# Attention and an expert layer: x times w_in from 7 block products of 384 tokens instead of 8

## The chip, the cores and the metric

The kernel runs on one core of a Trainium2 chip. The metric is the device time of one execution in microseconds. Engines are named as in the profile: PE (TensorE matmul), PEld (its weight load), DVE (VectorE), ACT (ScalarE), POOL (GpSimd), SP (SyncE, which issues the DMAs here).

## What is computed

```python
def _attn_ref(q, k, v, f):                       # batch 8, heads 8, 576 positions, 64 wide
    scores = scale * np.matmul(q, k.transpose(0, 1, 3, 2))
    cum = np.cumsum(np.log(np.clip(f, 0.0001, 1.0)), axis=-1)
    scores = np.where(causal, -1e9, scores + cum[..., :, None] - cum[..., None, :])
    attn = np.exp(scores - np.max(scores, axis=-1, keepdims=True))
    return np.matmul(attn / (np.sum(attn, axis=-1, keepdims=True) + 1e-09), v)

def _moe_ref(x, w_in, w_out):                    # x 4608 x 512, w_in 512 x 2048, w_out 2048 x 512
    h = x @ w_in
    sp = np.maximum(h, 0.0) + np.log1p(np.exp(-np.abs(h)))
    g = h * erf(sp)
    return g @ w_out
```

The attention's output, written as 4608 tokens of 512 values, is `x`. The weights arrive as 64-bit floats.

## The kernel before

The program has two stages. **The attention** works on half heads `t` = 0 to 63, five of them in flight, and writes the transposed output to the DRAM buffer `xt_d`. **The expert layer** (class `Moe`) follows; its first four units are already placed in the last attention steps. This change leaves the attention's own work alone.

Every number that enters a matmul of the expert layer is held as two float32r parts, a high part (`xh`, `wh`, `gh`) and the rest (`xl`, `wl`, `gl`), and a product is three matmuls: high x high, high x rest, rest x high. DVE or ACT makes the high part by a copy that rounds; POOL makes the rest by a subtraction.

A *unit* is one chunk of 512 tokens and 128 of the 2048 features. There are 9 chunks and 16 feature groups, so 144 units. `up` (L130) makes `h` of a unit in a PSUM bank, `ph`, from 12 matmuls of 512 columns (4 parts of the 512 inputs x 3). ACT then takes softplus of `ph` (L135) and erf (L138), DVE multiplies the result by `ph` (L144, one operand in PSUM) and rounds it (L146, a cast from SBUF to SBUF), and POOL makes the rest (L147). `down` (L168 to L170) then multiplies two units at a time with `w_out`: 24 matmuls of 512 columns into four PSUM banks `y`, which collect a visit's features. softplus and erf have different tables in ACT, so that each pair of units loads two tables (the load belongs to L138 and to L218).

The order on each engine is the order in which the code is written. `Moe.step` writes one unit: its `up`, then the `down` of an earlier pair, erf, softplus and the gates of earlier units, and the loads of `x`. Four PSUM banks hold `ph`, four hold `y`.

The weights are converted from 64-bit floats in pieces of 128 x 512 values: an Abs on ACT (L292), then DVE operations on SBUF (L296, L301, L303, L306), a cast (L309) and POOL's subtraction (L310). 16 pieces are converted in the attention stage, 16 beside the first part of the expert layer, two conversion steps in each `step`; the load of the next piece is issued when the last step of a piece is done (L282, through the SP queue). All converted weights stay in SBUF. The first five chunks are visited twice, each time with half of the features; their half sums go through DRAM (`part_d`).

## Time and profile before

| | us |
|---|---|
| median of 3 runs | 1117.68 (1116.02 to 1117.72) |
| the profiled execution | 1114.65 |
| its span, first to last instruction | 1112.9 |
| PE busy | 1102.9 (99% of the span) |
| DVE, ACT, POOL busy | 566.8, 694.2, 518.6 |
| first and last `up` matmul (L130) start | 312.0 and 1092.5 |

The profile is of one execution, and 1.8 us of its time lie outside its span. Rows of groups read: line, engine, operation, written tile <- read tiles, shape, count | busy us, mean ns of one | idle time before them, and what ended it. Rows of the timeline read: start, duration, engine, line. A query for one line or tile gives minimum, median and maximum in ns.

### The profile page before, as it was taken

The numbers are of one execution on the slowest core, as the hardware profiler recorded it, in microseconds if no ns is written. First come the engines' busy times: TensorE is split into PE (matmuls) and PEld (weight loads), VectorE is DVE, ScalarE is ACT, GpSimd is POOL, SyncE is SP. The second block draws the span as 40 slices with busy tenths as digits, with TensorE's granted clock in tenths as the row PEclk, the third lists the DMA queues.
The fourth block names the chain that finished last, engine by engine and source line by source line (L and its number), as shares of the span: only waits on it lengthen the run. The fifth ranks groups of instructions, "written<-read, shape, count | busy, mean of one in ns | idle before, by whom it ended". The sixth has DMA issues, their size and how long they took to land.

```text
span 1112.9 us, 19392 instructions
## 1 busy us (share of the span) xinstructions
PE 1102.9 (99%) x7096; PEld 914.8 (82%) x7096; DVE 566.8 (51%) x1475; ACT 694.2 (62%) x1303; POOL 518.6 (47%) x664
## 2 busy tenths in 40 slices
PE   8999999999999999999999999999999999999998
PEld 7888888888878888888888888888888888888887
DVE  6888888888855575764323332233223222313322
ACT  4888888888878697885554544554454445345442
POOL 4778787878945354354243242342232232223211
PEclk9999999999999999999999999999999999999999
DMA  8788787888613224131122032030011000000101
GB/s 289 215 259 265 238 258 250 261 250 252 213 63 104 78 77 133 62 109 57 46 87 95 19 114 95 19 114 38 1 38 39 1 24 30 24 19 1 39 1 38
DMA packets 57726, 120.03 MB, mean 108 GB/s; under 512 B 4768, under 2 KB 20128, under 8 KB 57632
## 3 DMA queue, kind: packets, MB, share of 16 engines
q1 hardware_dynamic: 57632, 118.80, 33.2%
q8 instruction: 56, 0.92, 0.3%
q14 instruction: 38, 0.31, 0.1%
HBM read 94.52 MB, written 24.26 MB: 107 GB/s over the span
## 4 chain that ended last, share of the span: by engine, by line
PE 96%; DVE 1%; issue 1%; ACT 1%; POOL 0%; POOLq 0%; DVEq 0%; ACTq 0%
PE ph L130 35%; PE y L170 12%; PE y L168 12%; PE y L169 12%; PE s L380 9%; PE o L461 8%; PE t L434 8%; DVE pr L400 1%; PE s L384 1%; PE idle L493 0%; ACT pr L412 0%; ACT pt L443 0%; POOL pr L422 0%; DVE pt L441 0%; POOL c L367 0%
## 5 line engine op out<-in xcount | busy, mean ns | idle before, releaser
L147 POOL TENSOR_TENSOR gl<-e,gh 128x512 fp32r<-128x512 f32 x144 | 186.2, 1293 | 410.0 <-DVE gh L146 403.2
L130 PE MATMUL ph<-xh,w 128*128 128x512 f32 x1152 | 367.3, 390 | 0.6 <-DVE st L400 0.6
L135 ACT ACTIVATE e<-ph 128x512 f32<-128x512 f32 x144 | 86.0, 598 | 278.9 <-PE ph L130 160.9
L130 PEld LDWEIGHTS ph<-xh,w 128*128 128x128 f32 x1152 | 216.2, 188 | 45.7 <-PE o L461 0.7
L144 DVE TENSOR_TENSOR e<-e,ph 128x512 f32<-128x512 f32 x144 | 98.3, 682 | 298.0 <-ACT e L138 298.0
L130 PE MATMUL ph<-xl,w 128*128 128x512 f32 x576 | 224.1, 389 | 0.0
L168 PE MATMUL y<-w,gh 128*128 128x512 f32 x576 | 224.1, 389 | 0.0
L169 PE MATMUL y<-w,gh 128*128 128x512 f32 x576 | 224.1, 389 | 0.0
L170 PE MATMUL y<-w,gl 128*128 128x512 f32 x576 | 224.1, 389 | 0.0
L422 POOL TENSOR_SCALAR pr<-pr,st 128x576 f32<-128x576 f32 (+4 forms) x320 | 165.5, 537 | 46.3 <-DVE st L418 38.4
L412 ACT ACTIVATE pr<-pr,st 128x576 f32<-128x576 f32 (+3 forms) x320 | 176.8, 558 | 4.8 <-DVE st L400 4.8
L400 DVE CUSTOM_DVE_ANT_0 pr<-s,c 128x576 f32<-128x576 f32 (+3 forms) x320 | 136.6, 486 | 37.2 <-PE s L384 28.9
L146 DVE CAST gh<-e 128x512 fp32r<-128x512 f32 x144 | 102.0, 708 | 57.8 <-PE y L169 44.3
L168 PEld LDWEIGHTS y<-w,gh 128*128 128x128 f32 x576 | 108.3, 188 | 22.5
L130 PEld LDWEIGHTS ph<-xl,w 128*128 128x128 f32 x576 | 108.2, 188 | 22.5
L170 PEld LDWEIGHTS y<-w,gl 128*128 128x128 f32 x576 | 107.9, 187 | 22.5
L169 PEld LDWEIGHTS y<-w,gh 128*128 128x128 f32 x576 | 108.1, 188 | 22.3
L380 PE MATMUL s<-k,q 64*128 64x320 f32 (+4 forms) x768 | 108.5, 407 | 2.1 <-DVE st L400 2.1
L434 PE MATMUL t<-ident,pr 128*128 128x128 f32 x800 | 104.4, 276 | 2.2 <-DVE pt L441 1.1
L443 ACT COPY pt<-t 128x512 f32<-128x512 f32 x128 | 73.6, 577 | 48.4 <-PE t L434 48.4
L461 PE MATMUL o<-pt,v 128*64 128x128 f32 (+1 forms) x1920 | 102.5, 259 | 0.0
L461 PEld LDWEIGHTS o<-pt,v 128*64 128x64 f32 x1920 | 93.7, 137 | 9.5 <-DVE st L400 4.9
(56 smaller groups left out, 1089.5 us busy)
## 6 DMA issues: line engine op xcount, KB each, us to landing
v<-in_vp_dram SPq DMA_DIRECT2D x32, 576.0 KB, 6.5
c<-cum_d SPq DMA_DIRECT2D x62, 288.0 KB, 5.3
xr<-xt_d SPq DMA_DIRECT2D x28, 512.0 KB, 3.4
q<-in_q_dram SPq DMA_DIRECT2D x32, 320.0 KB, 3.5
k<-in_k_dram SPq DMA_DIRECT2D x32, 288.0 KB, 4.0
xt_d<-xo SPq DMA_DIRECT2D x32, 288.0 KB, 5.6
wraw<-in_w_in_dram SPq DMA_DIRECT2D x16, 512.0 KB, 5.6
wraw<-in_w_out_dram SPq DMA_DIRECT2D x16, 512.0 KB, 4.4
```

The lines of the kernel that those rows point to most:

```text
L130: nc.tensor.matmul(out=ps, lhsT=w[:, kd, fs], rhs=x[:, kd], start=kd == 0 and n == 0, stop=kd == KD - 1 and n == 2)
L146: nc.vector.tensor_copy(out=gh, in_=e_)
L147: nc.gpsimd.tensor_tensor(out=gl, in0=e_, in1=gh.bitcast(F32), op=ALU.subtract)
L168: nc.tensor.matmul(out=y[tb], lhsT=gh[:, cs], rhs=wh, start=first, stop=False)
L169: nc.tensor.matmul(out=y[tb], lhsT=gh[:, cs], rhs=wl, start=False, stop=False)
L170: nc.tensor.matmul(out=y[tb], lhsT=gl[:, cs], rhs=wh, start=False, stop=last)
L380: nc.tensor.matmul(out=s[j][:, at:at + k1 - k0], lhsT=q[h, PAD + START[i]:PAD + END[i]], rhs=k[h, k0:k1], start=i > 0, stop=i not in (0, 3))
L400: nc.vector.tensor_tensor_reduce(out=to[:, ::-1] if j else to, in0=score, in1=decay_, scale=-0.125, scalar=BIG, op0=ALU.add, op1=ALU.min, ...
L412: nc.scalar.activation(out=seg, in_=seg, func=AF.Exp, bias=st[:, 0, j, m:m + 1], scale=-1.0, accum_out=st[:, 1, j, m:m + 1])
L422: nc.gpsimd.tensor_scalar(out=seg, in0=seg, scalar1=st[:, 2, j, m:m + 1], scalar2=1.0, op0=ALU.mult, op1=ALU.mult)
L434: nc.tensor.transpose(out=b[:, n * P:(n + 1) * P], in_=probs[t][:, at:at + P], identity=ident)
L461: nc.tensor.matmul(out=o[h, to:to + width], lhsT=v[:, ch, h], rhs=pt[:, at[j]:at[j] + width], start=n == 0, stop=n == len(parts) - 1, skip ...
```

## The change

The product x times w_in of two blocks of 384 tokens, two halves of the 512 inputs and two groups of 128 features is made by Strassen's scheme: 7 products of blocks instead of 8, on sums and differences of the blocks of x and of w_in. What follows is in the words of the new code.

A *block* is a pair of 384-token blocks with half of the features (1024); there are 6 pairs and 2 halves, first all pairs with the first half, then all with the second, so 12 blocks. A block has four *steps* (`k` = 0 to 3, `n` = 0 to 47 over all), each with 256 features. A step has seven *slots*. In slot `i` PE makes product `i`, 6 matmuls of 384 columns (2 input parts x 3), and then 5 (in the last slot 6) of the 36 `y` matmuls of 512 columns of step `n - 2`.

- `product` uses two PSUM banks in turn; products 2, 5 and 6 are added on to 0, 3 and 4 in their bank, and so must wait until `consume` has read what was there.
- `consume` brings each result to SBUF. After products 0 and 2 that is a copy on ACT, after the others an addition on DVE of the bank and an SBUF tile. The four quarters of `h` end up in SBUF.
- After product 0, ACT takes the last two softplus and the four erf of step `n - 1`; after product 1, DVE and POOL make its four gates. The multiplication in `gate` now has both operands in SBUF.
- `load_x`, `x_sum`, `split_x` and `last_sum` make the seven sums of x of the next block, each of 128 x 768 values, in steps 2 and 3 of a block and step 0 of the next. Each has one buffer for both parts.
- `weight_work` converts the weights and makes the seven sums of w_in. Ten of the 32 pieces are converted in the attention stage; the other 22 are written as 108 small work items, and `filler` places them in the slots of steps 2 to 18 by the table `FILL`. The second half's parts are stored to DRAM (`wi_d`, `wo_d`), and `reload` reads them back over the first half's in steps 20 to 25. The tile for a loaded piece (`raw`) has one buffer; the next load is issued in `join`.
- All half sums of `y` of the first half go through DRAM (`part_d`); there are six `y` banks.
- The first 14 products (steps 0 and 1) lie in the last four attention steps, between transposes.

```diff
-TB = 512
+TB = 384
+PRODUCTS = [(0, 0, True), (4, 1, True), (1, 0, False), (3, 1, True), (5, 0, True), (2, 1, False), (6, 0, False)]
+XSLOT = [0, 5, 1, 4, 6, 2, 3]
+FILL = [[1, 0, 1, 1, 2, 1, 2], [1, 0, 1, 1, 1, 1, 2], [0, 0, 0, 0, 0, 1, 2]]
+YCUT = [0, 5, 10, 15, 20, 25, 30, 36]
...
+    def x_sum(self, v, j):
+        t, sub = self.t[v], self.nc.gpsimd
+        if j == 0:
+            sub.tensor_tensor(out=t[4], in0=t[2], in1=t[3], op=ALU.add)
+        else:
+            sub.tensor_tensor(out=t[2], in0=t[0], in1=t[2], op=ALU.subtract)
+
+    def split_x(self, v, i):
+        t, r = self.t[v], XSLOT[i]
+        src = t[{0: 0, 5: 0, 1: 1, 4: 4, 6: 2, 2: 1, 3: 3}[r]]
+        x = self.x_tile(v, r)
+        h, l = x[:, 0], x[:, 1]
+        if i in (3, 4):
+            nc.scalar.copy(out=h, in_=src)
+        else:
+            nc.vector.tensor_copy(out=h, in_=src)
+        eng = nc.vector if i in (0, 4) else nc.gpsimd
+        eng.tensor_tensor(out=l, in0=src, in1=h.bitcast(F32), op=ALU.subtract)
+        if i == 0:
+            nc.vector.tensor_tensor(out=t[0], in0=t[4], in1=t[0], op=ALU.subtract)
+
+    def last_sum(self, v):
+        self.nc.vector.tensor_tensor(out=t[1], in0=t[1], in1=t[0], op=ALU.subtract)
...
+    def product(self, n, i):
...
+        w, bank, first = PRODUCTS[i]
+        ps = self.m[bank]
+        w, x = self.wi[v // NPAIR, k][:, w], self.x[v, XSLOT[i]]
+        for kd in range(2):
+            ws = slice(kd * P, kd * P + P)
+            for j, (wp, xp) in enumerate(((0, 0), (0, 1), (1, 0))):
+                nc.tensor.matmul(out=ps, lhsT=w[:, wp, ws], rhs=x[:, xp, kd], start=first and kd == 0 and j == 0,
+                                 stop=kd == 1 and j == 2 and i in (1, 2, 5, 6), skip_group_check=True)
...
+    def consume(self, n, i):
+        ps = self.m[PRODUCTS[i][1]]
+        if i == 0:
+            nc.scalar.copy(out=self.s1, in_=ps)
+        elif i == 1:
+            nc.vector.tensor_tensor(out=self.u2, in0=ps, in1=self.s1, op=ALU.add)
+        elif i == 2:
+            nc.scalar.copy(out=self.h_tile(n, 0), in_=ps)
+        elif i == 3:
+            nc.vector.tensor_tensor(out=self.u4, in0=ps, in1=self.u2, op=ALU.add)
+        else:
+            q, base = {4: (3, self.u4), 5: (1, self.u2), 6: (2, self.u2)}[i]
+            nc.vector.tensor_tensor(out=self.h_tile(n, q), in0=ps, in1=base, op=ALU.add)
...
+    def gate(self, n, q):
+        e, h = self.e.pop((n, q)), self.h.pop((n, q))
+        nc.vector.tensor_mul(e, e, h)
...
+        nc.vector.tensor_copy(out=gh, in_=e)
+        nc.gpsimd.tensor_tensor(out=gl, in0=e, in1=gh.bitcast(F32), op=ALU.subtract)
...
+    def step(self, n):
...
+        if gates:
+            self.softplus(n - 1, 0)
+            self.softplus(n - 1, 1)
+        if after and k == 2:
+            self.load_x(v + 1)
+        for i in range(7):
+            if up:
+                self.product(n, i)
+                self.consume(n, i)
+            if gates and i == 0:
+                for q in (2, 3):
+                    self.softplus(n - 1, q)
+                for q in range(4):
+                    self.erf(n - 1, q)
+            if after and k == HU - 1 and i < 2:
+                self.split_x(v + 1, i)
+            if gates and i == 1:
+                for q in range(4):
+                    self.gate(n - 1, q)
+            if up and i == (2 if gates else 5):
+                self.nc.scalar.preload_act_table_set(SOFTPLUS)
+            if after and k == HU - 1 and 2 <= i < 5:
+                if i == 3:
+                    self.last_sum(v + 1)
+                self.split_x(v + 1, i)
+            if up and v and k == 0 and i < 2:
+                self.split_x(v, 5 + i)
+            if after and k == 2 and i in (5, 6):
+                self.x_sum(v + 1, i - 5)
+            for _ in range(YCUT[i + 1] - YCUT[i]):
+                next(downs, None)
+            if n >= 2:
+                self.filler(FILL[0 if n < 5 else 1 + (k == HU - 1)][i])
...
+        for m, (a, i) in enumerate(pieces):
+            work += [lambda m=m: magnitude(m), lambda m=m: normal(m), lambda m=m: low_bits(m)]
+            if i >= 2:
+                work.append(lambda m=m: (join(m), out_parts(m)))
+            elif i == 0:
+                work.append(lambda m=m: (join(m), in_parts(m, 0, quarter(m, 0))))
+            else:
+                work += [lambda m=m: join(m), lambda m=m: [in_parts(m, 1 + f, quarter(m, f)) for f in range(2)],
+                         lambda m=m: sums(m, 0), lambda m=m: sums(m, 1)]
+                work += [lambda m=m, j=j: [in_parts(m, 3 + w, tops["t"][:, w]) for w in (j, j + 1)] for j in (0, 2)]
```

`magnitude` is the Abs on ACT, `normal`, `low_bits` (two instructions) and `join` are the DVE operations, `in_parts` and `out_parts` the cast on DVE and the subtraction on POOL, and where the piece is of the second half also two stores.

**PE.** Before, the matmuls of a pair of units stand in one piece, and so do those of `down` (the end of a `down` and the start of a unit, `ph`):

```order
L169 MATMUL y3_3_6602<-w3_108,gh31_6786 128x512
L170 MATMUL y3_3_6602<-w3_108,gl31_6787 128x512
L130 MATMUL ph36_6884<-xh4_6506,w2_107 128x512
L130 MATMUL ph36_6884<-xl4_6507,w2_107 128x512
L130 MATMUL ph36_6884<-xh4_6506,w2_107 128x512 x2
L130 MATMUL ph36_6884<-xl4_6507,w2_107 128x512
```

Now, in a step of block 9 (counted from 0), each product (`m39_*`, the banks of step 39) is six matmuls of 384 columns between five of `y9_*` of step 37:

```order
L147 MATMUL m39_1_11473<-x9_5_10927,wi1_3_9292 128x384 x6
L206 MATMUL y9_0_11353<-wo1_1_9294,gl37_1_11379 128x512
L206 MATMUL y9_1_11354<-wo1_1_9294,gh37_0_11373 128x512 x2
L206 MATMUL y9_1_11354<-wo1_1_9294,gl37_0_11374 128x512
L206 MATMUL y9_1_11354<-wo1_1_9294,gh37_1_11378 128x512
L147 MATMUL m39_0_11472<-x9_1_10964,wi1_3_9292 128x384 x6
L206 MATMUL y9_1_11354<-wo1_1_9294,gh37_1_11378 128x512
L206 MATMUL y9_1_11354<-wo1_1_9294,gl37_1_11379 128x512
```

A bank is now needed again two products later, where before a unit's bank came round after four units.

**DVE.** Before, the gates of two units stand alone on DVE for long stretches (L144 reads the bank `ph`):

```order
L144 TENSOR_TENSOR e56_7630<-e56_7630,ph56_7614 128x512
L146 CAST gh56_7700<-e56_7630 128x512
L144 TENSOR_TENSOR e57_7674<-e57_7674,ph57_7637 128x512
L146 CAST gh57_7746<-e57_7674 128x512
L196 TENSOR_TENSOR part6_0_7510<-y6_0_7506,part6_0_7510 128x512
```

Now, in the last step of a block (step 23), the sums of the next block's x (`x6_*`, `t6_*`) stand ahead of the gates of step 22:

```order
L121 CAST x6_0_9168<-t6_0_9000 128x768
L123 TENSOR_TENSOR x6_0_9168<-t6_0_9000,x6_0_9168 128x768
L125 TENSOR_TENSOR t6_0_9000<-t6_4_9004,t6_0_9000 128x768
L163 TENSOR_TENSOR sb23_9183<-m23_1_9151,sa23_9158 128x384
L121 CAST x6_5_9185<-t6_0_9000 128x768
L184 TENSOR_TENSOR e22_0_9146<-e22_0_9146,h22_0_9077 128x384
L188 CAST gh22_0_9189<-e22_0_9146 128x384
```

and, after the other three gates, between them and the additions that free the banks for products 5 and 6 (`sc23`, `h23_3`):

```order
L188 CAST gh22_3_9204<-e22_3_9162 128x384
L121 CAST x6_1_9222<-t6_1_9001 128x768
L168 TENSOR_TENSOR sc23_9237<-m23_2_9230,sb23_9183 128x384
L129 TENSOR_TENSOR t6_1_9001<-t6_1_9001,t6_0_9000 128x768
L171 TENSOR_TENSOR h23_3_9255<-m23_3_9248,sc23_9237 128x384
```

POOL's part of the same step: the rest of `x6_5` stands ahead of the four gates' rests, that of `x6_1` behind them:

```order
L123 TENSOR_TENSOR x6_5_9185<-t6_0_9000,x6_5_9185 128x768
L189 TENSOR_TENSOR gl22_0_9190<-e22_0_9146,gh22_0_9189 128x384
L189 TENSOR_TENSOR gl22_1_9195<-e22_1_9148,gh22_1_9194 128x384
L189 TENSOR_TENSOR gl22_2_9200<-e22_2_9160,gh22_2_9199 128x384
L189 TENSOR_TENSOR gl22_3_9205<-e22_3_9162,gh22_3_9204 128x384
L123 TENSOR_TENSOR x6_1_9222<-t6_1_9001,x6_1_9222 128x768
```

The additions out of PSUM, which come behind the gates in every step, have the sums of x between them and the gates in this one; `t6_1` is overwritten by DVE after POOL has read it.

**ACT.** Before, a weight piece's Abs (`wtop17`) stands behind the softplus of a unit, with a table load on either side:

```order
L218 ACT_TABLE_LOAD
L135 ACTIVATE e6_5669<-ph6_5653 128x512
L292 ACT_TABLE_LOAD
L292 ACTIVATE wtop17_5676<-wraw17_5651 128x512
L135 ACT_TABLE_LOAD
L135 ACTIVATE e7_5716<-ph7_5679 128x512
```

Now, at the change from step 8 to step 9, the Abs of piece 10 stands ahead of the softplus of step 8 (`e8_*`) and of the copy `sa9` of product 0 of step 9:

```order
L356 ACT_TABLE_LOAD
L356 ACTIVATE ltop10_6838<-lraw10_6817 128x512
L175 ACT_TABLE_LOAD
L175 ACTIVATE e8_0_6857<-h8_0_6777 128x384
L175 ACTIVATE e8_1_6859<-h8_1_6831 128x384
L160 COPY sa9_6869<-m9_0_6861 128x384
```

What waits for that copy is product 2 of step 9, which is added on in the same bank.

More of the change, by code (lines that the diff above doesn't have):

```diff
@@ L68, with __init__ @@
 class Moe:
[L75 to L77 removed]
+    def __init__(self, tc, xt_d, part_d, out, xs):
         self.tc, self.nc = tc, tc.nc
[L79 to L94 removed]
@@ L203, in more @@
-    def more(self):
-        return self.at < self.steps
-    def step(self):
-        j, n = self.at, len(self.units)
-        self.at += 1
-        if j < n:
-            self.up(j)
-            self.want_x(self.units[min(j + 5, n - 1)][0])
-        if self.downs[j]:
-            for i in range(0, len(self.downs[j]), 2):
-                self.down(self.downs[j][i:i + 2])
-        if j in self.ends:
-            for i in self.ends[j]:
-                self.erf(i)
-            self.nc.scalar.preload_act_table_set(SOFTPLUS)
-        if j < n:
-            self.softplus(j)
-        for i in self.gates[j]:
-            self.gate(i)
-        for i in self.downs[j]:
-            self.finish(i)
-        self.split_x()
-        self.load_x()
+        self.xt_d, self.part_d, self.out, self.xs = xt_d, part_d, out, xs
@@ new lines, in down @@
+    def down(self, n):
+        nc = self.nc
+        v, k = divmod(n, HU)
+        if k == 0:
+            self.y[v] = [self.ps_y.tile([P, DM], F32, name=f"y{v}_{tb}", tag=f"y{tb}") for tb in range(NTB)]
+        y, w = self.y[v], self.wo[v // NPAIR, k]
+        for tb in range(NTB):
+            token, at = divmod(tb, 3)
+            cs = slice(at * P, at * P + P)
+            for f in range(2):
+                gh, gl = self.g[n, 2 * token + f]
+                for j, (g, wp) in enumerate(((gh, 0), (gh, 1), (gl, 0))):
+                    first, last = k == 0 and f == 0 and j == 0, k == HU - 1 and f == 1 and j == 2
+                    yield nc.tensor.matmul(out=y[tb], lhsT=g[:, cs], rhs=w[:, f, wp], start=first, stop=last)
+            if k == HU - 1:
+                self.finish(v, tb)
@@ L284, in convert @@
-    def convert(u, step):
-        a, i = divmod(u, 4)
-        half, col = i // 2, slice(i % 2 * 512, i % 2 * 512 + 512)
-        raw = raws[u].rearrange("p (n w) -> p n w", w=2)
-        w0, w1_ = raw[:, :, 0], raw[:, :, 1]
-        if step == 0:
-            raws[u, 0] = top = cv.tile([P, 512], F32, name=f"wtop{u}", tag="wtop")
-            nc.scalar.activation(out=top, in_=w1_.bitcast(F32), func=AF.Abs)
-            return
-        top = raws[u, 0]
-        if step == 1:
-            nc.vector.scalar_tensor_tensor(out=top, in0=top, scalar=TINY, in1=w1_.bitcast(F32),
+    part_d = [dram.tile([P, DM], F32, name=f"part_d{c}") for c in range(NT // P)]
@@ L486, in attention_moe, with moe_products @@
         nc.sync.dma_start(out=fd[1], in_=f[0, 1].partition_broadcast(P))
-        todo = pieces[1]
+        tail = iter(i for n in range(2) for i in moe.step(n))
+        def moe_products(t, n):
+            if NH <= t < NH + 4:
+                for _ in range(n if t % 2 == 0 or n < 2 else 1):
+                    next(tail)
         def idle_products(t, n):
@@ L513, in attention_moe @@
                 load_values(p - 1)
-            if NH <= t < NH + 4:
-                moe.step()
             if there[2]:
@@ L530, in attention_moe @@
                     mask(0, slice(1, 2))
+            moe_products(t, 2)
             if there[3]:
```

377 lines of the change are left out of this document (215 added, 162 removed).

## The prediction

> **What bounds the kernel now.** I read the page first, then the stages, the chain and PE's waits.
>
> ```profile
> span 1112.9 us, 19392 instructions
> PE 1102.9 (99%) x7096; PEld 914.8 (82%) x7096; DVE 566.8 (51%) x1475; ACT 694.2 (62%) x1303; POOL 518.6 (47%) x664
> ```
> ```profile
> 343.00:1093.00 750.00, 750.00 (x3311) 621.02 (x3310) 281.48 (x410) 413.71 (x486) 260.97 (x181) 1.00 0.16 53
> ```
> ```profile
> 347.61 5.44 PE ph L130 x24
> ...
> 1087.45 5.44 PE ph L130 x24
> ```
> ```profile
> PE s L380 <- DVE st L400: 2.1, 2, 1.7
> ```
>
> PE is busy all through the expert layer, at the full granted clock (the 1.00), and the longest wait of PE anywhere is 1.7 us. From the first to the last quoted piece of the chain lie 739.84 us and 68 pairs of units, 10.88 us each. A pair has 48 matmuls of 512 columns: 226.7 ns each. So the layer costs 72 x 10.88 = 783.4 us of PE, and fewer columns are a real gain as long as PE stays fed. DVE and POOL have slack of many us here:
>
> ```profile
> DVE e L144 <- ACT e L138: 298.0, 50, 12.0
> ```
>
> **Term 1, fewer columns.** A step has 7 x 6 = 42 matmuls of 384 columns and 36 of 512; 48 steps replace the 72 pairs. No row has 384 columns. The nearest is 226.7 ns at 512: in proportion 170. The other side is the 128-column transposes:
>
> ```profile
> 203.65 1.48 PE L434 MATMUL t<-ident,pr 128*128 128x128 f32 x12
> ...
> L434 PE MATMUL t<-ident,pr x800: 270/273/328, 24.1 to 330.2; 128*128 128x128 f32 x160
> ```
>
> Twelve starts in 1.48 - 0.27 us are 110 ns each, and the line from there to 226.7 gives 188 at 384. I take 173, near the proportional end, since 110 is about the pace of loading 128 columns of weights and that hides under 170. A step is 42 x 0.173 + 36 x 0.2267 = 15.43 us, 48 are 740.5: **-42.9** (ends -49 and -13). The Trainium skill ("TensorE: Matmul & The Clock Gate", Back-to-back issue gap) gives columns / 2.4 + 2.5 ns, 162.5 ns at 384; by it this term would be -64. It gives 216 at 512 where the trace has 226.7, so the trace decides.
>
> **Who must keep pace.** Product 5 starts 5 x (6 x 0.173 + 5 x 0.2267) = 10.86 us after product 0, and needs bank 1 read by DVE (`consume` of 3), which stands behind the step's four gates. So I walk that queue, with these rows:
>
> ```profile
> L130 PE MATMUL ph<-xh,w 128*128 128x512 f32 x1152 | 367.3, 390 | 0.6 <-DVE st L400 0.6
> L147 POOL TENSOR_TENSOR gl<-e,gh 128x512 fp32r<-128x512 f32 x144 | 186.2, 1293 | 410.0 <-DVE gh L146 403.2 <-PE ph L130 3.4 <-PE t L434 3.4
> L118 POOL TENSOR_TENSOR xl<-xr,xh 128x1024 fp32r<-128x1024 f32 x28 | 67.9, 2425 | 53.4 <-ACT xh L117 52.4 <-DVE st L418 1.1
> L198 DVE COPY yo<-y 128x512 f32<-128x512 f32 x32 | 21.7, 689 | 42.7 <-PE y L170 31.5 <-DMA part_d<-yo 11.3
> L470 DVE COPY xo<-o 128x256 f32<-128x256 f32 x32 | 12.7, 398 | 0.0
> L138 ACT ACT_TABLE_LOAD x72 | 92.4, 1283 | 1.3
> L181 ACT COPY yo<-y 128x256 f32<-128x256 f32 x4 | 1.5, 372 | 11.3 <-DVE yo L179 11.3
> L443 ACT COPY pt<-t 128x512 f32<-128x512 f32 x128 | 73.6, 577 | 48.4 <-PE t L434 48.4
> ```
> ```profile
> L303 DVE SCALAR_TENSOR_TENSOR wraw<-wraw x32: 692/702/1667, 40.9 to 513.2; 128x512 int32<-128x512 int32 x32
> L306 DVE SCALAR_TENSOR_TENSOR wtop<-wtop,wraw x32: 681/698/1664, 45.5 to 513.9; 128x512 int32<-128x512 int32 x32
> ...
> L146 DVE CAST gh<-e x144: 426/430/1461, 328.6 to 1098.7; 128x512 fp32r<-128x512 f32 x144
> ```
> ```profile
> 357.57 1.15 ACT L138 ACTIVATE e<-e 128x512 f32<-128x512 f32 x2
> ...
> 356.37 1.31 POOL L147 TENSOR_TENSOR gl<-e,gh 128x512 fp32r<-128x512 f32 x1 [2.78 <-DVE gh L146]
> 356.57 1.66 DVE L303 SCALAR_TENSOR_TENSOR wraw<-wraw 128x512 int32<-128x512 int32 x1
> ...
> 359.33 0.68 DVE L144 TENSOR_TENSOR e<-e,ph 128x512 f32<-128x512 f32 x1
> 359.50 1.29 POOL L310 TENSOR_TENSOR w<-wtop,w 128x512 fp32r<-128x512 f32 x1 [1.82 <-DVE w L309]
> 360.14 0.93 DVE L146 CAST gh<-e 128x512 fp32r<-128x512 f32 x1
> ```
>
> Interpolated by size: DVE with two inputs 0.55 at 384 columns and 0.98 at 768; a cast 0.36 and 0.57 (at most in proportion to the 0.43); POOL 1.01 and 1.86; ACT 0.47, or 0.4 where one follows another (two erf of 512 took 1.15). A matmul's row lasts 390 ns at a pace of 227, so a result lands 0.16 after its turn. The last rows show the point that decides. DVE's L303, both inputs in SBUF, began inside POOL's 356.37 to 357.68 and ended at 358.23, 0.55 after POOL, in 1.66 us instead of 0.69; the cast at 360.14 ended 0.28 after POOL's 360.79; L144, with an input in PSUM, kept its 0.68 beside POOL. So DVE on SBUF alone and POOL take turns. `gate` now multiplies SBUF by SBUF, so that all it does takes turns with POOL. That is read from L303 and L306, which are scalar_tensor_tensor; the row with the same operation, L144, would let it run free. The Trainium skill ("SBUF — State Buffer", Who interferes with whom) says that a DVE instruction with two SBUF inputs contends with a POOL one that reads SBUF, tensor_tensor by name, as the walk has it; by L144's row alone the total below would be about 1120.
>
> *A plain step* (from product 0's start): product 0 has landed at 1.2, copied by 1.75, two softplus by 2.55 (overlapped), table 3.85, first erf 4.3; product and cast of the first gate 5.3. Each further gate costs 1.55: its product, during which POOL's rest of the gate before waits, then POOL's remaining 0.87, then the cast's remaining 0.2. The last cast ends at 10.0, the addition at 10.5: 0.35 before product 5 is due. No wait, and nothing to spare.
>
> **Term 2, the last step of a block.** Ahead of the gates DVE now has a cast, two sums of 768, an addition and a cast: 1.24 + 0.57 + 0.98 + 0.98 + 0.55 + 0.57, done at 4.8 (a little overlapped). POOL's rest of that cast (1.86) starts behind the first gate's product and ends at 7.0, the first gate's cast 7.2, the fourth 11.8, the cast of the next x 12.3, the addition 12.85: product 5 waits 2.0. Then `last_sum` overwrites what POOL still reads: the fourth gate's rest until 13.2, x's rest until 15.1, `last_sum` 16.1, the next addition 16.6, where product 6 was due at 15.0: 1.6 more. 3.6 us for each of 11 block changes: **+40**. If POOL begins its next 1.86 ahead of `last_sum`, as it may, the price is 5.2 (57); down to 0 if DVE does not stand in turn at all. I take the lower of the walked values.
>
> **Term 3, block ends.** One step in four also has `y` results to move: one DVE copy of 0.69 ahead of the addition in the first half (0.3 late), two in the second (1.0 late): 6 x 0.3 + 6 x 1.0 = **+8** (0 to 12).
>
> **Term 4, weights.** 108 items over steps 2 to 18. (a) One item stands between the gates and the addition: `low_bits` 0.43 + 0.69 with POOL between costs 1.4, `normal` 0.25, others about 1.2; 13 steps have one there, at 0.9: 12. (b) `raw` has one buffer, so that an Abs directly behind `join` waits for a whole load:
>
> ```profile
> DMA to landing us min/median/max: 3.5/3.7/4.8
> ```
> ```profile
> ACT L292 <- DMA wraw<-in_w_in_dram: 10.4, 3, 3.7
> ```
>
> (the first is L282 between 340 and 515 us). Before, that wait fell on ACT between units, 10.4 us in all, and PE had four banks. Now, where the Abs ends a step, the copy of product 0 (for product 2) and the first softplus stand behind it and a table load. At step 8 to 9: `join` done at 15.3, landed 19.0, Abs 19.7, table 20.95, softplus and copy 22.2, which is 5.1 into step 9 where product 2 is due at 4.35; the first erf is 3.3 late, the copy of `y` follows, and product 5 waits 2.7 more: 3.5. Four changes like that (into steps 9, 13, 15, 16) and three milder ones of 2 (into 3, 4, 5): 20. Together **+32**. Bounds: 0 if all falls into slack; 60 if all 17 steps cost 3.5.
>
> **Term 5, the attention's end.** In step 1, softplus, table and erf stand on ACT ahead of the copy that frees a transpose bank; after product 0: 0.3 + 0.4 + 0.8 + 1.3 + 1.5 + 0.6 = 4.9 us against PE's 2.3 of other work: **+2.5** (0 to 5). The conversion in the attention stage is 10 pieces instead of 16, in smaller casts, and I cost it at nothing, hidden by PE as now; so too the added DMA (weights out and back, x twice, `y` halves), since DMA is busy 16% in this stage.
>
> **Sum.** -42.9 + 40 + 8 + 32 + 2.5 = +39.6. On the profiled execution's 1114.65 that is 1154; the runs' median stands 3.0 above it, so I say **1155**, slower, with 0.2% (2.2 us) as what a measurement can tell from no change.
>
> **Rivals.**
> - *A, faster: taking turns costs little.* Terms 2 to 4 (80 us) all price DVE and POOL queueing for the same port at the end of a fixed chain; if POOL mostly finds DVE waiting for ACT, as in the 298 us above, they shrink together. For it: DVE is busy 281 of 750 us there. Against it: the gates of a step come back to back now. At half the price it is 1114.65 - 42.9 + 40 + 2.5 = 1114, the turning point; at a quarter 1094, and I give it as 1096 to 1117.
> - *B, steeper:* POOL goes ahead of `last_sum` (57) and the loads hold up most weight steps (50): -42.9 + 57 + 8 + 50 + 2.5 = +75, 1189. For it: POOL needs no signal to go on. Against it: a late step gives the next more time.
> - *C, 384 columns are not three quarters of 512:* at 188 ns Term 1 is -13 and the time 1184. For it the transposes, against it that they do a fixed load per 128 columns.
>
> **How the numbers follow.** My walk 0.53 (1125 to 1180), A 0.28, B 0.12, C 0.07. The range 1096 to 1190 leaves out a quarter of A's cases below and a part of B's and C's above, under 0.2. Faster by over 0.2% only in A below the turning point: 0.25; within 0.2%: 0.05; slower 0.70.
>
> **What would show it.** Term 1: 384-column matmuls 170 to 175 ns apart. Term 2: PE waiting on DVE at L147 about 2 us twice in each last step of a block, DVE's casts at L188 ending 0.2 us after POOL's L189, and L184 at over 1 us. Term 4: ACT waiting for `lraw`, and steps 2 to 18 longer than 24 to 40. I am wrong if PE stays over 97% busy in the layer, if L184 stays at 0.55 us beside POOL, or if a step without sums and weights takes over 16 us.

## The result: 1254.8 us, slower by 12%, and the profile after

| | before | after |
|---|---|---|
| median, us | 1116.85 (1114.75 to 1117.72, 4 runs) | 1254.76 (1250.91 to 1261.44, 4 runs) |
| span of the profiled execution, us | 1112.9 | 1254.0 |

After to before: 1.124, 95% interval 1.119 to 1.130. The prediction said 1155, slower; the sign was right and 100 us were missing.

The head of the page after:

```profile
span 1254.0 us, 21300 instructions
...
PE 1124.1 (90%) x7384; PEld 969.9 (77%) x7384; DVE 906.4 (72%) x1990; ACT 674.4 (54%) x1452; POOL 679.0 (54%) x808
...
PEclk8999999999998888998998899999999999999999
```

PE now stands idle for 10% of the span, and the granted clock, full all through before, falls in slices 13 to 23 (of 31.4 us each). The stages (start and end, length, then busy time of PE, PEld, DVE, ACT and POOL with counts, granted clock, DMA share, GB/s): attention up to the first expert matmul; steps 0 and 1; steps 2 to 18, with the weights' conversion; steps 19 to 46; step 47 and the end.

```profile
0.00:331.60 331.60, 314.65 (x3483) 262.46 (x3483) 279.15 (x1047) 248.86 (x772) 252.28 (x479) 0.98 0.70 221
331.60:362.10 30.50, 27.81 (x242) 25.66 (x243) 16.57 (x35) 15.14 (x31) 16.88 (x23) 0.94 0.12 40
362.10:732.60 370.50, 299.42 (x1328) 256.94 (x1327) 276.67 (x416) 184.49 (x276) 177.92 (x138) 0.91 0.31 101
732.60:1216.60 484.00, 449.91 (x2185) 397.27 (x2184) 316.09 (x465) 214.71 (x356) 222.85 (x161) 0.99 0.26 86
1216.60:1254.00 37.40, 32.29 (x151) 27.53 (x150) 17.90 (x28) 11.17 (x19) 9.05 (x8) 0.99 0.17 57
```

The first expert matmul comes at 331.6 us, where it came at 312.0, so 20 us are lost before the changed product does anything. Seventeen steps with weights take 370.5 us, 21.8 each. In the stage behind them I take the length of a step, from its first matmul to that of the next (worked out from the trace's records):

```
plain step (22, 26, 30, 34, 38, 42, 46)              15.75 us
last step of a block (23, 27, 31, 39, 43)            20.61 to 20.64 us
second step of a block in the second half (29, 33..) 16.6 us
steps 3, 4, 5                                        29.3, 26.9, 24.4 us
steps 6 to 18                                        15.8 to 26.6 us, 21.1 on average
```

What PE waited for (total, times, longest):

```profile
PE m L147 <- DVE sc L168: 47.2, 24, 5.5
PE m L147 <- DVE h L171: 25.9, 13, 2.8
PE y L206 <- DVE wo L383: 16.4, 3, 6.8
PE m L147 <- ACT sa L160: 12.1, 5, 2.8
PE o L596 <- DMA v<-in_vp_dram: 7.6, 3, 3.2
```

L168 is the addition that product 5 waits for, L171 the one that product 6 waits for, `wo` the freshly converted w_out, L160 the copy of product 0, and the last row is the attention.

The second place that the prediction walked through, the last step of a block (start, duration, engine, line):

```profile
878.10 0.55 DVE L184 TENSOR_TENSOR e<-e,h 128x384 f32<-128x384 f32 x1
878.25 1.27 POOL L189 TENSOR_TENSOR gl<-e,gh 128x384 fp32r<-128x384 f32 x1 [0.30 <-DVE gh L188]
878.68 1.06 DVE L188 CAST gh<-e 128x384 fp32r<-128x384 f32 x1
...
879.66 0.55 DVE L184 TENSOR_TENSOR e<-e,h 128x384 f32<-128x384 f32 x1
...
884.14 3.61 POOL L123 TENSOR_TENSOR x<-t,x 128x768 fp32r<-128x768 f32 x2
...
886.02 2.54 DVE L129 TENSOR_TENSOR t<-t,t 128x768 f32<-128x768 f32 x1 [2.23 <-POOL x L123]
888.48 0.55 DVE L171 TENSOR_TENSOR h<-m,sc 128x384 f32<-128x384 f32 x1
...
889.08 1.31 PE L147 MATMUL m<-x,wi 128*128 128x384 f32 x6 [2.76 <-DVE h L171]
```

The turns are there: POOL's subtraction ends at 879.52 and DVE's cast, 0.36 us when alone, at 879.74, 0.22 later; one gate follows another after 1.56 us. It is so in the whole trace: 155 of the 192 casts at L188 began inside a POOL instruction and took 1.11 us on average, the other 37 took 0.36. And `last_sum` (L129) costs more than walked: POOL does two rests of 768 back to back, `last_sum` waits 2.23 us for the first, begins at 886.02 beside the second, ends only 0.81 after that one, and PE's next product stands behind it all.

The clock. Its record changes on a grid of 3.413 us. Two neighbouring stretches of the grid in step 19:

```profile
744.67:748.08 3.41, 0.70 (x4) 0.70 (x5) 2.62 (x5) 0.00 (x0) 2.85 (x3) 1.00 0.00 0
748.08:751.50 3.41, 3.16 (x9) 2.17 (x7) 1.96 (x1) 0.00 (x0) 3.19 (x2) 0.50 0.00 0
```

PE was busy 0.70 of 3.41 us, and in the next stretch it got half the clock: 9 matmuls in 3.16 us.

### The profile page after: what moved, and what is told of

It is laid out like the page before. It is cut to its first block, busy times and chain, and to the rows that moved or that the text cites. A ratio compares the mean times of both kernels' runs of the same rounds, so it can differ in the third digit from the quotient of the medians.

```text
span 1254.0 us, 21300 instructions
## 1 busy us (share of the span) xinstructions
PE 1124.1 (90%) x7384; PEld 969.9 (77%) x7384; DVE 906.4 (72%) x1990; ACT 674.4 (54%) x1452; POOL 679.0 (54%) x808
## 5 line engine op out<-in xcount | busy, mean ns | idle before, releaser
L147 PE MATMUL m<-x,wi 128*128 128x384 f32 x2016 | 429.2, 349 | 87.0 <-DVE sc L168 47.2
L147 PEld LDWEIGHTS m<-x,wi 128*128 128x128 f32 x2016 | 372.1, 194 | 133.7 <-DVE sc L168 60.2
L206 PE MATMUL y<-wo,gh 128*128 128x512 f32 x1152 | 385.5, 403 | 18.6 <-DVE wo L383 16.4
L189 POOL TENSOR_TENSOR gl<-e,gh 128x384 fp32r<-128x384 f32 x192 | 228.1, 1188 | 296.5 <-DVE gh L188 270.5
L206 PEld LDWEIGHTS y<-wo,gh 128*128 128x128 f32 x1152 | 220.4, 193 | 53.8 <-DVE wo L383 17.7
L206 PE MATMUL y<-wo,gl 128*128 128x512 f32 x576 | 231.7, 402 | 0.0
L557 POOL TENSOR_SCALAR pr<-pr,st 128x576 f32<-128x576 f32 (+4 forms) x320 | 167.9, 545 | 58.6 <-DVE st L553 30.2
L188 DVE CAST gh<-e 128x384 fp32r<-128x384 f32 x192 | 186.1, 969 | 6.6
L123 POOL TENSOR_TENSOR x<-t,x 128x768 fp32r<-128x768 f32 x55 | 105.0, 1916 | 92.4 <-DVE x L121 85.7
L206 PEld LDWEIGHTS y<-wo,gl 128*128 128x128 f32 x576 | 111.5, 194 | 17.9
L184 DVE TENSOR_TENSOR e<-e,h 128x384 f32<-128x384 f32 x192 | 106.2, 553 | 22.0 <-ACT e L178 21.9
L171 DVE TENSOR_TENSOR h<-m,sb 128x384 f32<-128x384 f32 x96 | 53.0, 554 | 60.8 <-PE m L147 59.9
```

The source lines that it names most:

```text
L123: eng.tensor_tensor(out=l, in0=src, in1=h.bitcast(F32), op=ALU.subtract)
L147: nc.tensor.matmul(out=ps, lhsT=w[:, wp, ws], rhs=x[:, xp, kd], start=first and kd == 0 and j == 0, stop=kd == 1 and j == 2 and i in (1, 2 ...
L184: nc.vector.tensor_mul(e, e, h)
L188: nc.vector.tensor_copy(out=gh, in_=e)
L189: nc.gpsimd.tensor_tensor(out=gl, in0=e, in1=gh.bitcast(F32), op=ALU.subtract)
L206: yield nc.tensor.matmul(out=y[tb], lhsT=g[:, cs], rhs=w[:, f, wp], start=first, stop=last)
```

## The experiments

Medians are of 4 runs or more; each has its ratio to runs of the kernel before on the same chip (1114.8 to 1116.2 us). Experiments with several edits name the earlier ones they hold.

### e_xload: the loads of block 0's x

```diff
             for m, (token, half) in enumerate([(0, 0), (0, 1), (1, 0), (1, 1)]):
+                nc.gpsimd.memset(t[m][:, :, :1], 0.0)
                 for kd in range(2):
                     nc.sync.dma_start(out=t[m][:, kd], in_=moe.x_block(0, token, 2 * half + kd))
```

> Edit: in the attention's last part a one-column memset on POOL is written into each tile of block 0's x ahead of its loads, so that these loads (ta, tb <- xt_d) can be queued on SP only then, not right behind the first stores of xt_d. Theory: between t = 9 and 19 the attention lost 13.8 us because the early loads made the SP queue stand until stores had landed, with the loads of q, k, c and v behind them. Then these 13.8 us go, PE does not wait for v, the first expert matmul starts near 316 us instead of 331.6, and the time is 1238 to 1242. Rival: the converted weights' 512 KB loads crowd the DMA engines; then v is as late as now and the time stays at 1250 to 1256.

Measured: 1243.87 us, ratio 1.114 (1.112 to 1.117). SP's queue in the changed kernel, without this edit (timeline rows, then a row of its waits in the attention):

```profile
73.37 0.95 SPq L611 DMA_DIRECT2D xt_d<-xo  x1
82.48 0.32 SPq L443 DMA_DIRECT2D ta<-xt_d  x1
82.89 0.38 SPq L476 DMA_DIRECT2D q<-in_q_dram  x1
```
```profile
SPq L443 <- DMA xt_d<-xo: 62.3, 8, 8.9
```

The code writes these loads 8 half heads before the attention's end, but SP's queue is not in the hand-written order, and there they stood right behind the store that they read: eight times the queue stood still for up to 8.9 us, and q, k, c and v came late. With the edit the value matmuls of half head 19 start at 119.9 us, as before (119.8), not at 137.1, and the first expert matmul at 314.9. So the theory holds for the attention. The time is 2 us above the range: the median came down 10.9 us; the profile shows 16.7 at that point, of which 3.2 are a stretch of half clock near the start that the profile of e_xload does not have, and later there are some stretches of half clock more (four late last steps at 21.6 to 22.7 us, where the changed kernel had one).

### e_lastsum: last_sum behind product 6

```diff
-                if i == 3:
-                    self.last_sum(v + 1)
                 self.split_x(v + 1, i)
+            if after and k == HU - 1 and i == 6:
+                self.last_sum(v + 1)
```

> Edit: last_sum, which overwrites what POOL still reads, is moved from between products 3 and 4 of a block's last step to behind product 6's addition. Theory: the 3.0 us before product 6 are this wait, and the 1.8 us before product 5 are the four gates and the casts ahead. Then steps 19, 23, ... 43 take 17.5 instead of 20.6 us, the following step stays at 15.8, and 11 block changes give back 30 to 35 us: 1219 to 1225. Rival: DVE and POOL simply have too much to do there; then the wait moves to product 2 or 5 of the next step, which grows by 2 us or more, and the time is 1240 or higher.

Measured: 1223.42 us, 1.097 (1.095 to 1.100). Steps 23 to 43 take 17.61 instead of 20.63, the next ones are unchanged at 15.83, and L129's mean is 1.29 us instead of 2.55. As expected: the 3.0 us were this one instruction's place in the queue. Of the 32.5 us between the two profiles, 21 lie in steps 19 to 46 and 7 in steps 2 to 18; the other 5 lie ahead of the first expert matmul, where the edit changes nothing. That matmul starts at 326.5 to 335.8 us in the profiles of the changed kernel and of those experiments that leave the attention alone, so some us of a gain read from one profile can be chance.

### e_raw2: two buffers for the raw weights

```diff
-        ... {"raw": ("raw", 1), "top": ("top", 2), ...
+        ... {"raw": ("raw", 2), "top": ("top", 2), ...
-            load(m + 1)
+            load(m + ahead)          # 2 here, and two loads at the start
```

> Edit: two buffers for the raw weights, and each load issued one piece earlier. Theory: steps 2 to 18 take 370.5 us where plain steps and the last-step surcharge give 288, because ACT, with the softplus and the copy of product 0 behind its Abs, waits 97 us for loads of lraw; without that wait most of these 82 us go: 1180 to 1200, and few half-clock stretches remain between 350 and 750 us. Rival: the conversion's own work on DVE and POOL is what is late; then ACT's wait for lraw goes but PE waits as long, with DVE named: 1235 to 1255.

Measured: 1221.75 us, 1.096 (1.093 to 1.100), between the two. ACT's waits for the loads, three rows of the changed kernel,

```profile
ACT L356 <- DMA lraw<-in_w_out_dram: 34.9, 3, 13.7
ACT L356 <- DMA lraw<-in_w_in_dram: 29.3, 3, 12.2
ACT ltop L356 <- DMA lraw<-in_w_in_dram: 26.0, 2, 14.8
```

are gone, steps 2 to 18 take 332.7 instead of 370.5 us, and `y`'s wait for `wo` falls from 16.4 to 4.8. But PE still waits 39.2 us for L168, and these steps are still 45 us above 17 x 15.75 and four last-step surcharges.

### e_half_weights: no second half of weights

The second half of the features uses the first half's weights, so that part of the computation is changed; 16 of the 22 pieces are not converted, stored or loaded.

```diff
-        ... + [(a, i) for a in range(HU, NU) for i in range(4)], late_buf)
-    moe.reload = reload
+        ..., late_buf)
+    for k in range(HU):
+        moe.wi[1, k] = moe.wi[0, k]
```

> Edit: the 16 pieces of the second half's weights are not converted, stored or loaded back; the second half uses the first half's weights, so the output differs. Theory: everything by which steps 6 to 18 are longer than the later ones is this conversion, 54 us: 1198 to 1202, steps 6 to 18 at 15.8 and 20.6 like steps 20 to 46, with the clock full from step 6 on. Rival: a part of it is the clock, which was at half speed for 6.8 us at a time there, and does not come back with the conversion gone; then steps 6 to 10 stay over 17 us and the time is over 1210.

Measured: 1201.21 us, 1.077 (1.074 to 1.081). Steps 6 to 18 look like the later ones: 15.75 to 16.03, and 20.6 in last steps (22.1 in step 7). So all that made them longer was the conversion, with its loads and stores; steps 3, 4, 5 keep 29.3, 26.5, 25.0. (The full clock that was expected from step 6 on did not quite come: steps 31 and 43 took 22.3 and 21.8 us.)

### e_gh_on_act: DVE's cast moved to ACT

```diff
-        nc.vector.tensor_copy(out=gh, in_=e)
+        nc.scalar.copy(out=gh, in_=e)
```

> Edit: the high part of the gate (gh) is made by ACT's copy instead of DVE's cast; POOL's rest stays. Theory: DVE's casts take 0.97 us instead of 0.36 because each must let POOL's subtraction finish (they end 0.22 after it), so that the four gates hold DVE 6.2 us; without the casts they hold it 2.3 us, the 1.8 us before product 5 in the last steps and the 0.8 us in steps 29, 33, 37, 41 go, part of the 3.0 us before product 6 too, and about 30 us of the waits in steps 2 to 18: 1185 to 1215. Rival: the gates are late because their erf is late; then ACT, with 1.9 us more ahead of the copy of product 2, makes it worse: 1255 or more, with ACT named as what PE waits for.

Measured: 1217.10 us, 1.090 (1.087 to 1.093), 2 us above the range. The waits of the second steps (0.8) are gone, last steps take 19.6 us, steps 2 to 18 343.1. What is left is a new wait, the one that the rival named, in a result that is faster all the same:

```profile
PE m L147 <- ACT h L165: 33.9, 18, 4.1
```

The copy of product 2 stands behind the four copies of `gh` on ACT, and those wait for DVE.

### e_group_y: y in three groups

```diff
-YCUT = [0, 5, 10, 15, 20, 25, 30, 36]
+YCUT = [0, 0, 12, 12, 24, 24, 36, 36]
```

> Edit: the 36 matmuls of 512 columns of a step are placed in three groups of 12, behind products 1, 3 and 5, instead of seven groups of 5 or 6. Theory: back to back, 384-column matmuls start 173 ns apart and 512-column ones 227, but six of the one and five of the other in turn take 2.22 us where these give 2.17, so each change between the two widths costs 25 ns; four changes a step less twice over give 8 x 0.025 = 0.2 us: plain steps of 15.55 us in place of 15.75. Rival: the slower pace comes from what DVE, POOL and the DMAs do beside it; then m and y stay at means of 181 and 231 ns. In both, product 5 is due 0.2 us earlier and may wait as long, so the time says little: 1235 to 1260.

Measured: 1238.39 us, 1.109 (1.108 to 1.111). The plain step takes 15.66, half of the saving expected. The records of the changed kernel's last step, where `y` follows `y`, show why: behind a change of width the starts are late for several matmuls, not for one (384 columns: 177, 185, 176, 182, then 173 ns apart; 512: 229, 234, 236, 224, 231, 235, 229, 232, 231, then 227). Groups of five cut such a run off; long ones let it run out. That the width is the cause holds: before, with 512 columns throughout, the change from `ph` to `y` costs nothing (227 throughout). The time fell by 16.4 us all the same, most of it outside the plain steps: last steps take 19.4 instead of 20.6, and steps 2 to 18 take 362.3 instead of 370.5. Which wait that was this run alone does not show; e_fill_group comes back to it.

### e_three and e_four: together

e_three is e_xload, e_lastsum and e_raw2; e_four adds e_gh_on_act.

> Edit: the late x loads, the moved last_sum and the two raw buffers together. Theory: they are separate causes, and their gains (10.9, 31.3 and 33.0 us) add up: 1175 to 1185, still slower than the kernel before. Rival: they share stretches of half clock or cover one another's waits; then 1190 or more.

> Edit: the three and gh on ACT. Theory: what is left after the three (the gates' turns, 1.8 us in last steps, and the conversion's waits in steps 3 to 17) is mostly the turns of DVE's casts with POOL: 1130 to 1150, with PE waiting under 40 us in all after the attention. Rival: the weights are late by their own work; then steps 2 to 18 stay 25 us or more above 288 and the time is over 1155.

Measured: e_three 1177.84 us, 1.055 (1.052 to 1.058): the three gains add up to 75.2, and 76.9 came. e_four 1162.55, 1.042 (1.040 to 1.044): 12 us above the range, with steps 2 to 18 at 312.1 us, 24 above 288, and 30.2 us of PE's waits for ACT's L165.

### e_five, e_six, e_seven, e_eight: what ACT and the conversion still hold up

e_five is e_four with the gates behind product 2's copy; e_six converts two more pieces of w_out in the attention; e_seven is e_six with e_group_y; e_eight is e_six with the items spread.

```diff
-            if gates and i == 1:                               # e_five
+            if gates and i == 2:
...
-            for _ in range(1 + (t % 10 == 0)):                 # e_six
+            for _ in range(1 + (t % 4 == 0)):
...
-FILL = [[1, 0, 1, 1, 2, 1, 2], [1, 0, 1, 1, 1, 1, 2], [0, 0, 0, 0, 0, 1, 2]]     # e_eight
+FILL = [[0, 0, 0, 0, 0, 1, 1], [1, 1, 1, 1, 1, 2, 2], [1, 1, 1, 1, 1, 2, 2], [0, 0, 0, 0, 0, 1, 1], [0, 0, 0, 0, 0, 2, 2]]
```

> Edit: as e_four, and the gates are written behind product 2's copy on ACT, not ahead of it. Theory: what PE still waits for in e_four is ACT's copy of product 2, 30.2 us, behind the four copies of gh; with the order turned the last steps come down from 17.9 to about 16 us, steps 7, 11, 15, 19 from 21 to 24 to about 18, and with the half clock that follows such waits 28 to 35 us go: 1127 to 1136. Rival: the gates then end too late for the down product of the next step, or the additions of products 3 and 4 wait behind them on DVE; then PE waits there instead and the time is over 1145.

> Edit: as e_five, and the two pieces of w_out that step 3 needs first are converted in the attention, whose conversion takes two turns every fourth t instead of every tenth; tc moves to another slot. Theory: steps 3 to 5 of e_four take 64.5 us for 47.3 us of matmuls because y waits for w_out that is loaded only when the attention's buffers are free; with a step more of time 10 to 15 of these 17 us go: 1114 to 1124. Rival: the attention, with DVE busy 85 to 90%, gets slower by what the expert layer gains; then the first expert matmul starts 5 us or more later than at 316 and the time stays within 5 us of e_five.

> Edit: as e_six, with the y matmuls in three groups of 12. Theory: a plain step takes 15.65 instead of 15.75 us, 46 steps give 4.6 us, and no wait comes in with it now that DVE has room: 1109 to 1120, 4 to 5 below e_six. Rival: product 5 falls due earlier and waits; then e_six's time or more.

> Edit: as e_six, and the conversion's items are spread by where DVE has room: nine in each second and third step of a block, two in the first and in the last (four in steps 3 and 4) instead of 7 or 8, 7, 7 and 3. Theory: in e_six steps 3, 4, 7, 8, 11, 12, 15, 16 take 39 us more than 15.75 each, because there DVE and POOL also split x, while steps 5, 6, 9, 10, 13, 14, 17, 18 take 15.75 with 7 items in them; so 20 to 32 us go: 1112 to 1124. Rival: nine items are too many for a plain step; then steps 5, 6, 9, 10 and so on grow to 18 us or more and the time stays over 1130.

| | median, us | ratio | steps 2 to 18, us | a late last step, us |
|---|---|---|---|---|
| e_four | 1162.55 | 1.042 (1.040 to 1.044) | 312.1 | 17.91 |
| e_five | 1158.02 | 1.036 (1.035 to 1.038) | 321.2 | 16.53 |
| e_six | 1144.12 | 1.024 (1.023 to 1.026) | 308.0 | 16.53 |
| e_seven | 1149.12 | 1.029 (1.027 to 1.030) | 312.8 | 16.78 |
| e_eight | 1148.26 | 1.031 (1.029 to 1.033) | 305.1 | 16.54 |

e_five mended the last steps (16.53) and gave most of it back in steps 2 to 18, where PE then waits for DVE: the rival was right there. e_six gained 14 us, as expected in size, but from a worse start and not where it was expected: steps 3 to 5 gave 4 us (67.4 to 63.4), though PE no longer waits for `wo`, and steps 6 to 18 gave 9; the first expert matmul comes 5 us later (322.8), as the rival had it. e_seven and e_eight were misses, both slower than e_six: the items' place hardly matters, steps 2 to 18 stay 37 to 45 us over 17 x 15.75.

### e_x_on_dve, e_x_w_on_dve, e_all_on_dve, e_gl_after: turns, or too much work for DVE

Left open was why steps 2 to 18 stay long. All four are e_six with POOL's work given to DVE, step by step.

```diff
-        eng = nc.vector if i in (0, 4) else nc.gpsimd          # e_x_on_dve
+        eng = nc.vector if v or i in (0, 4) else nc.gpsimd
...
-            nc.gpsimd.tensor_tensor(out=vl, in0=src, ...       # e_x_w_on_dve, expert layer only
+            nc.vector.tensor_tensor(out=vl, in0=src, ...
...
-        nc.gpsimd.tensor_tensor(out=gl, in0=e, ...             # e_all_on_dve; in e_gl_after
+        nc.vector.tensor_tensor(out=gl, in0=e, ...             # behind all four products
```

> Edit: as e_six, and the rests and sums of x in the expert layer are made by DVE instead of POOL. Theory: DVE's operations on SBUF and POOL's use one port in turn, and POOL holds it about 1.9 us for what DVE does in 0.95; so steps 3, 4, 7, 8, 11, 12, 15, 16, where both split x and convert weights, get shorter although DVE is given 6.7 us more in each block change: 10 to 20 us off e_six, 1124 to 1134. Rival: DVE has too much to do; then PE waits longer for DVE and the time is 1144 or more.

> Edit: as e_x_on_dve, and the rests of the weights converted in the expert layer on DVE too, so that POOL only makes gl there. Theory: the same, 0.7 us on DVE for 1.3 of the port's turns on POOL, 20 pieces: 5 to 10 us off e_x_on_dve: 1116 to 1128. Rival: longer than e_x_on_dve, since nothing of this lay on PE's path or DVE is full.

> Edit: as e_x_w_on_dve, and gl on DVE too: POOL has nothing to do in the expert layer. Theory: there are no turns left, each operation of DVE takes what it takes alone (0.36, 0.55, 0.69, 0.95 us), and DVE's sum in steps 2 to 18 is about 264 of 283 us, so that the waits nearly go: 1105 to 1120. Rival: the port was not what held it; DVE with 40 to 50 us more work in these steps makes them longer than e_six's 324 us, and the time is over 1145.

> Edit: as e_all_on_dve, but DVE makes the four products of the gates first and the four gl after them, so that it does not wait for ACT's gh between them. Theory: without POOL there are no turns, and what made e_all_on_dve slow was DVE's 143.6 us of waiting for ACT's gh; a plain step has 2.75 + 2.2 + 2.2 us of DVE work and comes back to 15.75: 1120 to 1135 in all. Rival: with the conversion too DVE is full; steps 2 to 18 stay over 18 us each: 1160 or more.

| | median, us | ratio | steps 2 to 18, us | DVE, POOL busy, us |
|---|---|---|---|---|
| e_six | 1144.12 | 1.024 (1.023 to 1.026) | 308.0 | 816.6, 684.6 |
| e_x_on_dve | 1127.63 | 1.010 (1.008 to 1.013) | 289.8 | 820.7, 530.9 |
| e_x_w_on_dve | 1128.72 | 1.011 (1.009 to 1.013) | 290.2 | 833.6, 492.8 |
| e_all_on_dve | 1269.34 | 1.135 (1.133 to 1.138) | 353.7 | 872.8, 273.5 |
| e_gl_after | 1121.02 | 1.004 (1.002 to 1.005) | 284.8 | 859.3, 272.7 |

154 us of POOL's work went to DVE in e_x_on_dve, and DVE's busy time rose by 4 us only: its busy time had held waiting for turns. The trace shows how much. In e_six 68 of the 192 products at L184 began inside a POOL instruction and took 1.66 us on average, ending 0.42 after POOL; the other 124 took 0.55. The additions at L168, with an operand in PSUM, took 0.55 in either case. Summed over DVE's operations of the expert layer, what they took beyond their time alone (that of the quickest twentieth of each kind) is 141 us in e_six, 78 in e_x_on_dve and 5 in e_gl_after. (The range was 1124 to 1134.) In e_all_on_dve the edit itself made a chain, so it told nothing of the turns:

```profile
DVE gl L189 <- ACT gh L188: 143.6, 192, 3.6
```

e_gl_after has the same instructions without that wait. The rows of e_x_w_on_dve, where POOL still makes `gl`, and then of e_gl_after:

```profile
L184 DVE TENSOR_TENSOR e<-e,h 128x384 f32<-128x384 f32 x192 | 112.3, 647 | 12.0 <-ACT e L178 11.8
L123 DVE TENSOR_TENSOR x<-t,x 128x768 fp32r<-128x768 f32 x77 | 84.5, 1098 | 1.9
```
```profile
L184 DVE TENSOR_TENSOR e<-e,h 128x384 f32<-128x384 f32 x192 | 94.1, 553 | 10.5 <-ACT e L178 10.5
L123 DVE TENSOR_TENSOR x<-t,x 128x768 fp32r<-128x768 f32 x77 | 73.6, 956 | 1.9
L190 DVE TENSOR_TENSOR gl<-e,gh 128x384 fp32r<-128x384 f32 x192 | 94.2, 553 | 11.4 <-ACT gh L188 11.0
```

With POOL out of the expert layer DVE's operations take what they take alone, and the time is 7.7 us lower although DVE does 94 us more. (`gl` also stands behind all four products now, so the 7.7 us are not the turns' alone.) Of the 37 us by which e_six's steps 2 to 18 stand over plain and last steps, 19 went with e_x_on_dve and 3 more with e_gl_after, while DVE was given more to do: that part was the turns, not DVE's load. The last 15 stay where there are no turns left, and what they are is open. (e_x_w_on_dve showed no gain of its own, where 5 to 10 us were expected.)

### e_fill_shift and e_fill_group: a version that is not slower

Both are e_x_on_dve with fewer conversion items in last steps (1 instead of 3) and each split of x one product later; e_fill_group has e_group_y's YCUT too.

```diff
-                self.split_x(v + 1, i)
+                self.split_x(v + 1, i - 1)
```

> Edit: as e_x_on_dve; step 3 and the other last steps of a block get fewer conversion items, first and second steps more; each split of x is written one product later. Theory: in e_x_on_dve the steps 3, 4, 7, 11, 15, 16 take 19.5 us over 15.75 each and the later last steps 0.95 each, 7 times; one cast and one subtraction of 768 less (1.5 us) stand ahead of the addition that product 5 needs, so the 0.95 go and half of the 19.5: 1109 to 1118. Rival: the waits move to product 6 or to the next step's product 2, and it stays at 1124 to 1130.

> Edit: as e_fill_shift, with the y matmuls in three groups of 12. Theory: 15.65 us for a plain step, 4 to 5 us under e_fill_shift and under the kernel before: 1104 to 1114. Rival, as in e_seven: product 5 is due 0.2 us earlier and the waits that remain grow by as much as is gained.

Measured: e_fill_shift 1131.93 us, 1.014 (1.013 to 1.016); e_fill_group 1113.78 (1111.89 to 1116.75, 10 runs; before 1115.99, 14 runs), 0.9982 (0.9971 to 0.9994). The shift alone was a miss: last steps went from 16.71 to 17.57, since DVE now stands idle at a step's start, where the first split was, until product 1's result (3.3 us at step 27). With the grouped `y` that result comes 1.1 us earlier (the five `y` between products 0 and 1 are gone), last steps take 15.70 and plain ones 15.64: 18 us under e_fill_shift, four times what the grouping was expected to give, and 14 under e_x_on_dve. The busy times of e_fill_group, and PE's longest group of waits:

```profile
PE 1082.1 (97%) x7384; PEld 949.1 (85%) x7384; DVE 820.2 (74%) x1875; ACT 750.0 (67%) x1638; POOL 527.8 (47%) x735
```
```profile
PE m L147 <- DVE sc L168: 9.4, 6, 3.0
```

So the scheme with 7 products is at best 2 us faster here than the one with 8; PE has 20.8 us less to do, but stands idle 20.9 us more: 10.3 us up to the first expert matmul (4.3 before), 2.7 in steps 0 and 1, 12.8 in steps 2 to 18, none in steps 19 to 46 and 5.1 at the end.

## Why the prediction was wrong in size

| term | predicted | in the profile after | how |
|---|---|---|---|
| 1, fewer columns | -42.9 | -27.4 | 48 x (15.75 - 1.5 x 10.88) |
| 2, last steps | +40 | +54 | 11 x (20.63 - 15.75) |
| 3, block ends | +8 | +6 | steps 20 to 46 that are not last ones |
| 4, weights | +32 | +83 | 370.5 - 17 x 15.75 - 4 x 4.88 |
| 5, attention's end | +2.5 | +2.7 | PE's wait in step 1 |
| loads in the attention | 0 | +13.8 | half heads 9 to 20 against before |
| half clock at the start | not there | +3.2 | start of half head 0 |
| sum | +39.6 | +135 | the spans differ by 141 |

The remaining 6 us are half clock in steps 19 and 35 (3) and what I could not place. The sum's own end has a slip of 2 us: 1154 and 3.0 are 1157, not 1155.

- **Term 4 is the largest error (51 us).** Part (b) saw the mechanism, ACT waiting for a whole load, but priced seven steps at 2 to 3.5 us. ACT waited 97 us in ten places (three of its four rows stand with e_raw2), the longest 14.8, not the 3.7 of one load: the load is issued when `join` is done, and that was late already, so each wait made the next. The two buffers took 38 of the 83 us; of the rest a good part went when POOL's work on x was given to DVE (e_x_on_dve), and some 15 us never went. What I missed beside it: `y` in steps 3 to 5 needs w_out just converted; these three steps are 28 us too long, and PE waits 18.6 us there for `wo`.
- **A wait was priced at its length.** In the expert layer 153 matmuls ran at half the clock, 320 ns apart for 384 columns and 427 for 512, instead of 173 and 227: 85 x 0.147 + 68 x 0.200 = 26 us, most of it in Term 4's steps. The prediction has no step for this; before, PE never waited, so its profile does not show it.
- **"The added DMA at nothing"** failed. It rested on DMA being busy 16%, a mean of the wrong stage, and on bandwidth; what counted was the order in SP's queue, where each of these loads stands right behind a store (e_xload).
- **Term 1**: 173 ns apart was right back to back; a step is 15.75 instead of 15.43 because of the mixed widths, 15 us in all.
- **Term 2**: product 5's wait was right (2.0 walked, 1.8 measured). Product 6's was 3.0, not 1.6, since POOL took its next rest ahead of `last_sum`: rival B's mechanism, 5.2 us a change there, 4.9 measured.
- **The turns** were read rightly from L303 and L306: casts 0.22 us after POOL's end (0.2 said), gates 1.56 apart (1.55), no plain step over 16. But of the signs I named, "L184 over 1 us" was wrong and against my own walk, and by the other one, "if L184 stays at 0.55 us beside POOL", the turns would be refuted, which they are not. L184 stays at 0.55 because only 2 of its 192 instructions began inside one of POOL's: DVE begins first, and POOL is the one that waits. L189 takes 1.19, and 1.02 in e_fill_group, where `gh` is ACT's. In e_six, where POOL often begins first, it is L184 that waits. The Trainium skill ("SBUF — State Buffer", Who interferes with whom) says that the order of issue decides who blocks, and this trace agrees.
- **Rival A** fell: Terms 2 to 4 came to 143 us, not to half of 80, and e_x_on_dve shows that the turns are not cheap (16.5 us). **Rival B** had both of its mechanisms right, POOL ahead of `last_sum` and the loads, but took Term 4 at 50 where it came to 83, had no term for the clock and the attention, and so stopped at 1189. **Rival C** had the direction right for a wrong reason: Term 1 shrank to -27 (it said -13), not by the width but by the change of width.

## What to carry to other kernels

Where PE was never idle, price a new wait by where it ends on the clock's grid, not by its length alone: in e_lastsum the last steps' waits of 1.8 us never cost the clock, while those of 3.0 us did in one of six last steps after, and in four of six in e_xload. In a fixed order the cheapest repairs were places in a queue (a load behind its store, a sum behind another engine's reads, a copy behind a copy), and each repair has to be followed to the next engine that it makes late. Work that DVE and POOL share may be quicker on DVE alone, and a busy time that includes waiting for a turn does not show how much room there is.

## What the runs showed of the hardware

- **The clock goes by a grid of 3.413 us.** Over the profiles of the changed kernel and the 18 experiments, 226 stretches at full clock were followed by one at half: in 221 of them PE was busy for less than 0.48 of the stretch, in the other five for 0.54 to 0.58 (four of these five lie in the first 15 us). Of the 6014 that kept the clock none was busy for less than 0.42, and 18 for less than 0.48. So 2 us without a matmul inside one stretch cost the next one half its speed each time, less than 1.4 us never did, and between the two it went either way. A stretch lost in this way costs some 1.6 us of matmuls (3.41 x (1 - 173/320)). The Trainium skill ("TensorE: Matmul & The Clock Gate", What's actually happening) puts the return to half rate behind at least one idle window of about 3.4 us; the window agrees, but here it need not be idle, only some half busy or less.
- **At half clock the fixed part of a matmul disappears:** 320 and 427 ns are 384 and 512 columns at 1.2 per ns; at full clock, with twice that rate, 173 and 227 are 13 ns more than the columns take.
- **Matmuls of 384 and 512 columns in turn** cost 49 ns for six of one and five of the other over what they take alone, 0.34 us a step.
- **SP's queue waits for a store to land before a load of the same DRAM buffer**, up to 8.9 us here, with all later loads behind it.
- **DVE on SBUF alone and POOL take turns, and who begins first does not wait.** Casts, products and subtractions of DVE that began inside a POOL instruction ended 0.22 to 0.82 us after it; additions with an operand in PSUM kept their 0.55. DVE's busy time includes the waiting.
